# Plain first products in each MoE layer, sums of x made in the MoE, and two weight parts converted in single steps through the attention

## The chip, the cores and the metric

The kernel runs on one core of a Trainium2 chip. The metric is the device time in microseconds of one execution, the median of several. TensorE (PE) multiplies matrices and accumulates in PSUM; VectorE (DVE), ScalarE (ACT) and GpSimd (POOL) work element by element; SyncE (SP) issues DMAs, and so does POOL here. Each engine takes its instructions in the order in which they were written to its queue.

## What is computed

```python
scores = 0.125 * q @ k.T + bias(w1, b1, w2)      # 2 batches, 8 heads, 576 positions, head size 64
attn = softmax(scores); x = (attn @ v) as 1152 tokens x 512
x = ((x @ w_a) * (x @ w_b)) @ w_out              # first MoE layer, 512 -> 1536 -> 512
x = (silu(x @ w_gate) * (x @ w_val)) @ w_out2    # second MoE layer
```

The MoE weights arrive as 64-bit floats, which the kernel turns into 32-bit ones on the chip. All products keep 32-bit accuracy by splitting an operand into a high and a low part (`h` and `l` at the end of a name) and making three matmuls: high by high, high by low, low by high (`three`).

## The kernel before

**Attention.** The 1152 tokens are worked off in 20 steps: five row tiles t in the order 4, 0, 1, 2, 3, each for four pairs of heads p. A step of t=4 has one half step, the others two (one for each batch), so there are 36 half steps, counted here from 0. In each loop turn i, `first(i)` makes the scores in the PSUM tile `ps` (a single one), DVE adds the bias and finds the row extreme (the `es<-ps,bt` instruction, two in a half step), ACT takes the exponential; `second(i-1)` transposes on PE; `third(i-2)` multiplies by v, and `finish` scales the result by the inverse sums and splits it into x, high and low. Until turn 17 the loop also makes the position bias (`units`); then the pools of that work close and a pool for the weights opens in their place.

x has three token chunks of 384 (c = 0, 1, 2): `x0` (all four blocks of 128 rows), `x1` (blocks 2 and 3 only) and `x2`. For chunks 0 and 1 the MoE does not make eight block products but seven, after Winograd's scheme for 2 by 2 blocks; it needs four sums of x (`xt`, for two row pairs k) and four sums of weight blocks (`st`, the second half of `wh` and `wl`). In the attention `differences` makes `xt` on POOL, six elementwise operations and one subtraction of the high part at each of four places, with one ACT cast.

**Weights.** `Weights.part(layer, q, i)` fetches 1 MB (i = 0: w_a or gate, 1: w_b or value, 2: out) and converts it: ACT takes the absolute value, DVE makes four passes over 128x1024 elements (`m`), ACT casts the high part, DVE subtracts for the low part. For i below 2 DVE also makes the four sums (`s`), ACT casts them and DVE subtracts once more. `raw` and `m` have two buffers each; the high and low weights of i = 0 and i = 1 have one buffer each. Part (0,0,0) is made at the start of step 17 of the attention and part (0,0,1) at the start of the MoE in the program's text; DVE, ACT and POOL instructions are placed by a scheduler, which moved most of both into the last ten half steps.

**MoE.** Each layer has six q, each q two parts i of products. `products` makes the seven block products for chunks 0 and 1 in PSUM tiles `pa`, `pb`, `pd` with five DVE additions (`sum_of`); `plain` makes chunk 2 in `pv`. Between them `project` multiplies finished hidden values by the out weights into `po0` to `po3`, and DVE adds these to `acc`. `gate` copies on ACT, `value` multiplies and splits. PE's order is that of the program. At the end of layer 0, `project` empties its list of ten pieces, and `split` makes the new x from `acc`: casts on ACT, low parts on POOL, the four sums on DVE.

The order of the seven block products in `products`, which sets when PE needs `xt`, is: `x0` block, then `xt`[1], `xt`[0], `xt`[2], `x0`, `xt`[3], `x1`.

Of the kernel before, what the change touches and what calls it, by code (L numbers as in the profile page):

```python
# [2 lines left out]

# [6 lines left out]
F32 = mybir.dt.float32  # L10
F32R = mybir.dt.float32r
# [32 lines left out]
GROUP = 4  # L44
RAWS, MS, WOS, HS, GS, CS = 2, 2, 3, 12, 7, 3
# [27 lines left out]
class Activations:  # L73


    def __init__(self, pool):
        self.pool, self.late = pool, None
        self.layer()

    def layer(self):  # L80
        t = lambda n, tag: [self.pool.tile([P, n, CH], F32R, tag=f"{tag}{s}", name=f"{tag}{s}") for s in "hl"]
        self.x0, self.x1, self.x2 = t(NCC, "x0"), t(2, "x1"), t(NCC, "x2")
        if self.late:
            self.sums()
# [157 lines left out]
class Weights:  # L242
# [6 lines left out]
    def __init__(self, tc, wm, early):  # L249
        self.nc, self.early, self.pool, self.more, self.wm = tc.nc, early, None, None, wm  # L250
        self.got = {}

    def part(self, layer, q, i):
        nc = self.nc
        if i < 2:
            s, pool = i, (self.early, self.more)[i]
            wh, wl = (pool.tile([P, 8, 256], F32R, tag=f"w{x}{s}", name=f"w{x}{s}", bufs=1) for x in "hl")
        else:
            wh, wl = (self.more.tile([P, 4, 256], F32R, tag=f"wo{x}", name=f"wo{x}", bufs=WOS) for x in "hl")
        self.got[layer, q, i] = wh, wl  # L260
        raw = self.pool.tile([P, 2048], U32, tag="raw", name="raw", bufs=RAWS)
        nc.sync.dma_start(raw, self.wm[layer][q, i].bitcast(U32))
        lo, hi = (raw.rearrange("p (n t) -> p t n", t=2)[:, j] for j in range(2))
        mt = self.pool.tile([P, 4, 256], F32, tag="m", name="m", bufs=MS)
        m = mt.rearrange("p k f -> p (k f)")
        nc.scalar.activation(m, hi.bitcast(F32), AF.Abs)
        nc.vector.tensor_scalar(m, m, LEAST, MOST, op0=ALU.max, op1=ALU.min)
        t = m.bitcast(U32)
        nc.vector.tensor_scalar(t, t, 3, 0x3FFFFFF8, op0=ALU.logical_shift_left, op1=ALU.bitwise_and)
        nc.vector.scalar_tensor_tensor(t, lo, 29, t, op0=ALU.logical_shift_right, op1=ALU.bitwise_or)  # L270
        nc.vector.scalar_tensor_tensor(t, hi, 0xC0000000, t, op0=ALU.bitwise_and, op1=ALU.bitwise_or)  # L271
        nc.scalar.copy(wh[:, :4], mt)  # L272
        nc.vector.tensor_tensor(wl[:, :4], mt, wh[:, :4].bitcast(F32), op=ALU.subtract)  # L273
        if i < 2:
# [6 lines left out]
            nc.vector.tensor_tensor(wl[:, 4:], st, wh[:, 4:].bitcast(F32), op=ALU.subtract)  # L281


def attention(ctx, tc, a4, heads, share, bias, units, bias_d, x, weights, ident):
# [3 lines left out]
    with (  # L288
# [83 lines left out]
        def finish(p, s0, n, pu, rc):  # L372
            t1 = a2.tile([P, 256], F32, tag="t1", name="t1", bufs=4)
            nc.vector.tensor_tensor(t1[:, :n], pu[:, :n], rc[:, :n], op=ALU.mult)
            share.dve(n)
            share.dve(n)
            share.act(n)
            for c in range(NCH):
                a, e = max(s0, CH * c), min(s0 + n, CH * c + CH)
                if a >= e:  # L380
                    continue
                src, cols = t1[:, a - s0 : e - s0], slice(a - CH * c, e - CH * c)
                if c == 1:
                    kept[p] = src
                    if p < 2:
                        continue
                dh, dl = ((x.x0, x.x1, x.x2)[c][i][:, p - 2 if c == 1 else p, cols] for i in range(2))
                nc.scalar.copy(dh, src)
                nc.vector.tensor_tensor(dl, src, dh.bitcast(F32), op=ALU.subtract)
                if c == 1:  # L390
                    differences(p - 2, cols)

        def differences(k, cols):

            w = cols.stop - cols.start
            y0, y1 = kept[k], kept[k + 2]
            a, b = ([x.x0[i][:, r, cols].bitcast(F32) for i in range(2)] for r in (k, k + 2))
            tt = a4.tile([P, 4, 256], F32, tag="tt", name="tt", bufs=1)
            t = [tt[:, j, :w] for j in range(4)]
            add = nc.gpsimd.tensor_tensor  # L400
            add(t[0], y0, a[0], op=ALU.subtract)
            add(t[0], t[0], a[1], op=ALU.subtract)
            add(t[2], y1, y0, op=ALU.subtract)
            add(t[1], y1, t[0], op=ALU.subtract)
            add(t[3], b[0], t[1], op=ALU.subtract)
            add(t[3], t[3], b[1], op=ALU.add)
            dh, dl = (x.t[i][:, :, k, cols] for i in range(2))
            nc.scalar.copy(dh, tt[:, :, :w])
            nc.gpsimd.tensor_tensor(dl, tt[:, :, :w], dh.bitcast(F32), op=ALU.subtract)

        kept = {}
# [14 lines left out]
        def first(i):  # L426

            idx, p, t, b = halves[i]
            if b == 0:
# [41 lines left out]
        for i in range(len(halves) + 2):  # L471
# [20 lines left out]
def moe(tc, x, weights, out):  # L492
    nc = tc.nc
    pe = Pinned(tc, nc.tensor)
    with (
# [5 lines left out]
        weights.more = wpb  # L501
        weights.part(0, 0, 1)
        acc = [mp.tile([P, NCC, CH], F32, tag=f"acc{c}", name=f"acc{c}") for c in range(NCH)]
# [25 lines left out]
        def products(layer, q, i):  # L529
# [16 lines left out]
            product(a, 0, [v[:, :2] for v in x.x0], True)  # L546
# [11 lines left out]
            product(a, 1, [v[:, 2:] for v in x.x0], False)  # L558
# [5 lines left out]
            product(d, 7, x.x1, False)  # L564
# [3 lines left out]
        def plain(layer, q, i, j):  # L568
            w = weights.got[layer, q, i]
            ps = ph.tile([P, CH], F32, tag="pv", name="pv")  # L570
            for cc in range(NCC):
                ws = slice(P * (cc % 2), P * (cc % 2) + P)
                three(ps, [v[:, 2 * j + cc // 2, ws] for v in w], [v[:, cc] for v in x.x2], cc == 0, cc == NCC - 1)
            (gate, value)[i](layer, 2 * q + j, 2, ps, True)

        def project(layer, f0, f1, c, fc):
# [17 lines left out]
            if f1 == NFC and not layer:  # L594
                if c == 0:
                    x.layer()
                split(c)

        def split(c):
            dst = (x.x0, x.x1, x.x2)[c]  # L600
            for d in range(2 if c == 1 else 0, NCC):
                dh, dl = (v[:, d - 2 if c == 1 else d] for v in dst)
                nc.scalar.copy(dh, acc[c][:, d])
                nc.gpsimd.tensor_tensor(dl, acc[c][:, d], dh.bitcast(F32), op=ALU.subtract)
            if c == 1:
# [102 lines left out]
```

## Time and profile before

| | us |
|---|---|
| median of 3 runs | 683.8 (682.9 to 686.06) |
| the profiled execution | 688.58 |
| its span | 686.8 |
| PE busy | 630.1 (92%) |
| DVE busy | 557.0 (81%) |
| ACT busy | 347.8 (51%) |
| POOL busy | 50.2 (7%) |
| mean granted TensorE clock | 0.96 |

The profiled execution took 1.78 us more than its span from the first to the last instruction. Busy time of PE overstates its work, since matmuls overlap: the 128x384 ones show 0.34 us each and start every 0.17 us when nothing holds them up. So the number of matmuls in a stretch tells more than PE's busy time.

### The profile page before, as it was taken

The page shows a single profiled execution, that of the slowest core. Times are in us where ns is not written, and L with a number is a line of the kernel's source. Part 1 is how long each engine was busy: PE and PEld are TensorE (multiplying, and loading weights), DVE is VectorE, ACT ScalarE, POOL GpSimd, SP SyncE. Part 2 cuts the span into 40 slices and gives each one's busy share as a digit, 9 for nine tenths or more (in the row PEclk, how much of TensorE's full clock was granted, in tenths as well). Part 3 has the DMA queues.
Part 4 walks back from the last instruction along what each step waited for, and adds up shares of the span by engine and source line. Part 5 has one row for each costly group of instructions (what it writes and reads, how often), then busy time and mean ns, then how long its engine had stood idle before and what let it go on. Part 6 is the DMA issues. An engine that isn't in the chain of part 4 may idle for free.

```text
span 686.8 us, 11386 instructions
## 1 busy us (share of the span) xinstructions
PE 630.1 (92%) x4440; PEld 562.2 (82%) x4440; DVE 557.0 (81%) x1055; ACT 347.8 (51%) x672; POOL 50.2 (7%) x70
## 2 busy tenths in 40 slices
PE   5496999998958899999999999898999999999997
PEld 2254666577846799899999999788998999999997
DVE  6565789888879799989798989995999998887452
ACT  5486789875855644453544333444445445343210
POOL 4000000126230000000000000212000000000000
PEclk9789899998968999999999999998999999999999
DMA  8454364541444031333231312111113223110012
GB/s 326 169 181 149 114 187 138 155 138 57 126 167 163 36 124 61 123 112 113 84 123 62 108 52 86 62 62 62 63 61 123 72 113 123 62 62 1 0 47 93
DMA packets 19911, 71.42 MB, mean 104 GB/s; under 512 B 2096, under 2 KB 3776, under 8 KB 15248
## 3 DMA queue, kind: packets, MB, share of 16 engines
q1 hardware_dynamic: 17824, 63.21, 27.4%
q0 software_dynamic: 2032, 7.47, 3.2%
q8 instruction: 35, 0.57, 0.3%
q14 instruction: 20, 0.16, 0.1%
HBM read 57.42 MB, written 13.25 MB: 103 GB/s over the span
## 4 chain that ended last, share of the span: by engine, by line
PE 65%; DVE 19%; ACT 7%; DMA 5%; issue 3%; SPq 1%; ACTq 0%; DVEq 0%
PE po L98 20%; PE pv L98 12%; PE pb L98 9%; PE tp L98 6%; PE pd L98 6%; PE pa L98 5%; PE pu L98 4%; PE ps L98 3%; DMA bias_d<-bt 2%; ACT es L322 2%; DVE m L270 1%; ACT ee L329 1%; DVE m L271 1%; DVE wl L273 1%; ACT hd L155 1%
## 5 line engine op out<-in xcount | busy, mean ns | idle before, releaser
L98 PE MATMUL po<-gh,woh 128*128 128x384 f32 x288 | 97.4, 338 | 3.4 <-DVE acc L591 3.4
L98 PE MATMUL po<-gl,woh 128*128 128x384 f32 x288 | 97.2, 338 | 2.5 <-DVE gl L526 2.5
L98 PE MATMUL po<-gh,wol 128*128 128x384 f32 x288 | 97.0, 337 | 0.0
L525 ACT CAST gh<-g 128x384 fp32r<-128x384 f32 x72 | 35.2, 513 | 76.7 <-DVE g L523 76.5
L98 PE MATMUL tp<-hd,cs 128*32 128x264 f32 (+17 forms) x352 | 51.4, 551 | 18.1 <-DVE hd L153 15.4
L98 PE MATMUL pv<-x2h,wh 128*128 128x384 f32 x192 | 64.5, 336 | 0.4 <-ACT g L518 0.4
L316 DVE CUSTOM_DVE_ANT_0 es<-ps,bt 128x576 f32<-128x576 f32 x72 | 51.7, 751 | 15.6 <-DMA bt<-bias_d 10.0
L98 PE MATMUL pv<-x2l,wh 128*128 128x384 f32 x192 | 64.2, 334 | 0.0
L98 PE MATMUL pv<-x2h,wl 128*128 128x384 f32 x192 | 64.1, 334 | 0.0
L322 ACT ACTIVATE es<-es,nm 128x576 f32<-128x576 f32 x72 | 55.7, 775 | 9.0 <-DVE nm L316 8.8
L98 PEld LDWEIGHTS po<-gh,woh 128*128 128x128 f32 x288 | 54.6, 189 | 4.1 <-DVE acc L591 4.0
L98 PEld LDWEIGHTS po<-gl,woh 128*128 128x128 f32 x288 | 54.6, 190 | 3.6 <-DVE gl L526 3.5
L98 PEld LDWEIGHTS po<-gh,wol 128*128 128x128 f32 x288 | 54.5, 189 | 0.0
L98 PE MATMUL tp<-ident,es 128*128 128x128 f32 x324 | 48.7, 292 | 6.1 <-ACT es L322 3.9
L98 PE MATMUL pb<-xtl,wh 128*128 128x384 f32 x144 | 49.3, 343 | 4.2 <-DVE xtl L613 4.2
L98 PE MATMUL pb<-xth,wh 128*128 128x384 f32 x144 | 49.5, 344 | 2.8 <-DVE u L541 2.7
L98 PE MATMUL pu<-ee,vv 128*64 128x128 f32 (+1 forms) x800 | 51.6, 283 | 0.0
L98 PEld LDWEIGHTS tp<-hd,cs 128*32 128x32 f32 x352 | 14.2, 121 | 44.3 <-DVE hd L153 20.4
L98 PEld LDWEIGHTS tp<-ident,es 128*128 128x128 f32 x324 | 36.5, 147 | 15.9 <-ACT es L322 5.7
L272 ACT CAST wh<-m 128x1024 fp32r<-128x1024 f32 x24 | 25.3, 1052 | 47.9 <-PE pd L98 44.9
L98 PE MATMUL pb<-xth,wl 128*128 128x384 f32 x144 | 49.4, 343 | 0.0
L98 PEld LDWEIGHTS pu<-ee,vv 128*64 128x64 f32 x800 | 43.0, 148 | 6.3 <-issue 5.1
(124 smaller groups left out, 1512.4 us busy)
## 6 DMA issues: line engine op xcount, KB each, us to landing
raw<-in_wm SPq DMA_DIRECT2D x36, 1024.0 KB
bias_d<-bt SPq DMA_DIRECT2D x36, 295.5 KB
bt<-bias_d SPq DMA_DIRECT2D x32, 288.0 KB
vv<-in_vd POOLq DMA_DIRECT2D x4, 640.0 KB, 10.4
kr<-in_kd POOLq DMA_DIRECT2D x4, 576.0 KB, 7.3
bt<-bias_d SPq DMA_DIRECT2D x16, 144.0 KB
out_t<-acc SPq DMA_DIRECT2D x12, 192.0 KB
rawq<-in_qd POOLq DMA_DIRECT2D x16, 128.0 KB, 5.5
```

Source lines behind the costliest of these rows:

```text
L98: return self.tc.keep_in_program_order(getattr(self.engine, name)(*args, **kwargs))
L155: self.nc.scalar.activation(dst, self.LW[:, :n], AF.Relu, bias=self.bp[:, m : m + 1])
L270: nc.vector.scalar_tensor_tensor(t, lo, 29, t, op0=ALU.logical_shift_right, op1=ALU.bitwise_or)
L271: nc.vector.scalar_tensor_tensor(t, hi, 0xC0000000, t, op0=ALU.bitwise_and, op1=ALU.bitwise_or)
L272: nc.scalar.copy(wh[:, :4], mt)
L273: nc.vector.tensor_tensor(wl[:, :4], mt, wh[:, :4].bitcast(F32), op=ALU.subtract)
L316: nc.vector.tensor_tensor_reduce(out=es[:, j].rearrange("p (a j) -> p a j", a=2), in0=ps[:, j, :, :288], in1=bt[j].rearrange("p (a j) -> p ...
L322: nc.scalar.activation(es[:, j], es[:, j], AF.Exp, bias=nm, scale=-1.0, accum_out=sums[:, j : j + 1])
L329: nc.scalar.copy(dst, src)
L525: nc.scalar.copy(gh, g)
```

## The change

The diff has four parts.

- **Plain products.** For five (layer, q, i), named in `PLAIN`, chunks 0 and 1 are made like chunk 2, by `plain` with 72 matmuls in place of 66, going round `pa`, `pb`, `pd`, `pv`. These parts need no `xt` and no weight sums, and their weight part makes none.
- **Sums of x.** `differences` is gone. `x1` now has all four blocks, and `finish` keeps the unsplit result of chunks 0 and 1 in `acc0` and `acc1`, which now exist from the start. `sums`, which layer 1 had already, makes `xt` on DVE and ACT in layer 0 too, after part (0,0,0).
- **Weights ahead.** The raw data of parts (0,0,0) and (0,0,1) are fetched in turn 17. Their conversion is cut into twelve single instructions (five words, two split, five words), one put into each loop turn from 20 to 31 and pinned there.
- **Order.** `split(0,0,1)` comes at the start of the MoE; the parts for q = 1 are queued behind it.

```diff
+PLAIN = {(0, 0, 0), (0, 0, 1), (0, 1, 0), (1, 0, 0), (1, 0, 1)}
...
+        yield nc.scalar.activation(m, hi.bitcast(F32), AF.Abs)
+        yield nc.vector.tensor_scalar(m, m, LEAST, MOST, op0=ALU.max, op1=ALU.min)
+        yield nc.vector.tensor_scalar(t, t, 3, 0x3FFFFFF8, op0=ALU.logical_shift_left, op1=ALU.bitwise_and)
+        yield nc.vector.scalar_tensor_tensor(t, lo, 29, t, op0=ALU.logical_shift_right, op1=ALU.bitwise_or)
+        yield nc.vector.scalar_tensor_tensor(t, hi, 0xC0000000, t, op0=ALU.bitwise_and, op1=ALU.bitwise_or)
...
+        yield nc.scalar.copy(wh[:, :4], mt)
+        yield nc.vector.tensor_tensor(wl[:, :4], mt, wh[:, :4].bitcast(F32), op=ALU.subtract)
+        if i < 2 and (layer, q, i) not in PLAIN:
...
-                with tc.issue_after(load.ins):
-                    if idx == len(steps) - 3:
-                        weights.part(0, 0, 0)
...
-                weights.pool = x.late = ctx.enter_context(tc.tile_pool(name="wpa2", bufs=1, side="right"))
-                x.sums()
+                weights.pool = ctx.enter_context(tc.tile_pool(name="wpa2", bufs=1, side="right"))
+                weights.fetch(0, 0, 0)
+                weights.fetch(0, 0, 1)
+                ahead = chain(weights.words(0, 0, 0), weights.split(0, 0, 0), weights.words(0, 0, 1))
+            if i > len(MADE) + 1:
+                for op in islice(ahead, 1):
+                    units.tc.keep_in_program_order(op)
...
-            product(d, 7, x.x1, False)
+            product(d, 7, [v[:, 2:] for v in x.xs[1]], False)
...
+                    if (layer, q, i) in PLAIN:
+                        for n in range(2 * NCH):
+                            plain(layer, q, i, n % 2, n // 2, ("pa", "pb", "pd", "pv")[n % 4])
+                    else:
...
+                    if (layer, q, i) == (0, 0, 0):
+                        sums()
```

**DVE in the attention.** These are consecutive rows of DVE between the scores of half steps 30 and 31 in the kernel before. `m`, `s` and `wl` belong to the conversion of weights; `es` are the scores' instructions.

```order
L271 SCALAR_TENSOR_TENSOR m<-raw,m 128x1024
L269 TENSOR_SCALAR m<-m 128x1024
L367 COPY rc<-tp 128x256
L276 TENSOR_TENSOR s<-m 128x256
L278 TENSOR_TENSOR s<-m 128x256
L270 SCALAR_TENSOR_TENSOR m<-raw,m 128x1024
L273 TENSOR_TENSOR wl_2710<-m,wh_2709 128x1024
L277 TENSOR_TENSOR s<-s,m 128x256
L271 SCALAR_TENSOR_TENSOR m<-raw,m 128x1024
L279 TENSOR_TENSOR s<-m,s 128x256
L208 CAST qa<-rawq 128x256
L316 ISA es,nm<-ps,bt 128x576
```

And these are rows of DVE in the changed kernel between two half steps of the same part of the attention.

```order
L342 COPY ee<-tp 128x384
L382 COPY rc<-tp 128x256
L270 SCALAR_TENSOR_TENSOR m<-raw,m 128x1024
L209 CAST qa<-rawq 128x256
L331 ISA es,nm<-ps,bt 128x576
```

Nine conversion rows stood between two scores before; now one stands there, and there is never more than one.

**SP in the attention.** The DMA queue of SP around the last steps, before: `bt` is the bias of a step read back, `raw` a weight part.

```order
L194 DMA bias_d_60<-bt 16x8x591
L433 DMA bt<-bias_d_59 128x1x576 x6
L433 DMA bt<-bias_d_60 128x1x576 x4
L262 DMA raw<-in_wm 128x2048 x2
L433 DMA bt<-bias_d_60 128x1x576 x2
L262 DMA raw<-in_wm 128x2048 x2
```

In the changed kernel:

```order
L195 DMA bias_d_60<-bt 16x8x591
L256 DMA raw<-in_wm 128x2048 x2
L425 DMA bt<-bias_d_59 128x1x576 x6
L256 DMA raw<-in_wm 128x2048
L425 DMA bt<-bias_d_60 128x1x576 x8
```

The first two weight parts are now issued ahead of the last fourteen bias loads, which are seven steps' worth (six of tile 2, eight of tile 3), and a third stands between them.

**DVE at the change of layer.** Before, when the last pieces of chunk 0 come out of PSUM (`po`) at the end of layer 0:

```order
L591 TENSOR_TENSOR acc_3154<-po_4921,acc_3154 128x384
L267 TENSOR_SCALAR m<-m 128x1024
L276 TENSOR_TENSOR s<-m 128x256
L278 TENSOR_TENSOR s<-m 128x256
L591 TENSOR_TENSOR acc_3154<-po_4922,acc_3154 128x384
```

In the changed kernel:

```order
L585 TENSOR_TENSOR acc_73<-po_4886,acc_73 128x384
L268 TENSOR_SCALAR m<-m 128x1024
L585 TENSOR_TENSOR acc_73<-po_4887,acc_73 128x384
```

The two sums of weights are no longer ahead of the fourth addition; one pass over 128x1024 still is.

## Rows read from the trace of the kernel before

**Rows 1.** The page: busy time, share of the span and instructions of each engine.

```profile
PE 630.1 (92%) x4440; PEld 562.2 (82%) x4440; DVE 557.0 (81%) x1055; ACT 347.8 (51%) x672; POOL 50.2 (7%) x70
```

**Rows 2.** Windows by stage: busy time and instructions, granted clock, DMA.

```profile
core 0: us, PE busy (x) PEld busy (x) DVE busy (x) ACT busy (x) POOL busy (x), PEclk, DMA share, GB/s
147.00:235.00 88.00, 73.55 (x758) 60.19 (x759) 71.77 (x168) 59.19 (x139) 24.33 (x31) 0.86 0.36 116
234.00:300.00 66.00, 60.56 (x338) 58.25 (x337) 62.78 (x100) 28.39 (x42) 0.00 (x0) 1.00 0.27 96
300.00:436.00 136.00, 136.00 (x782) 135.88 (x782) 121.56 (x197) 56.42 (x85) 0.00 (x0) 1.00 0.27 93
436.00:480.00 44.00, 36.30 (x182) 34.82 (x181) 34.03 (x49) 17.52 (x31) 12.03 (x10) 0.88 0.13 49
```

**Rows 3.** DVE's timeline: the first scores of half steps 20, 25, 29, 33 and 35.

```profile
151.56 0.74 DVE L316 CUSTOM_DVE_ANT_0 es<-ps,bt 128x576 f32<-128x576 f32 x1
...
174.91 0.76 DVE L316 CUSTOM_DVE_ANT_0 es<-ps,bt 128x576 f32<-128x576 f32 x1 [1.05 <-PE ps L98]
...
189.27 0.76 DVE L316 CUSTOM_DVE_ANT_0 es<-ps,bt 128x576 f32<-128x576 f32 x1 [0.96 <-PE ps L98]
...
220.38 0.74 DVE L316 CUSTOM_DVE_ANT_0 es<-ps,bt 128x576 f32<-128x576 f32 x1
...
227.31 0.76 DVE L316 CUSTOM_DVE_ANT_0 es<-ps,bt 128x576 f32<-128x576 f32 x1 [1.14 <-PE ps L98]
```

**Rows 4.** POOL's and DVE's timelines, 155 to 177 us: two DVE operations, slow and normal.

```profile
154.99 2.37 POOL L409 TENSOR_TENSOR xtl<-tt,xth 128x1024 fp32r<-128x1024 f32 x1 [1.95 <-PE tp L98]
...
155.90 1.75 DVE L212 TENSOR_TENSOR qb<-rawq,qa 128x256 fp32r<-128x256 f32 x1
...
176.27 0.42 DVE L212 TENSOR_TENSOR qb<-rawq,qa 128x256 fp32r<-128x256 f32 x1
```

**Rows 5.** ACT's, DVE's and SP's timelines: the first weight part in the attention.

```profile
184.27 0.81 SPq L262 DMA_DIRECT2D raw<-in_wm  x2
...
193.35 1.12 ACT L266 ACTIVATE m<-raw 128x1024 f32<-128x1024 f32 x1 [4.33 <-DMA raw<-in_wm]
...
194.50 0.70 DVE L267 TENSOR_SCALAR m<-m 128x1024 f32<-128x1024 f32 x1 [3.79 <-ACT m L266]
...
205.04 1.21 DVE L270 SCALAR_TENSOR_TENSOR m<-raw,m 128x1024 uint32<-128x1024 uint32 x1
206.18 1.21 DVE L273 TENSOR_TENSOR wl<-m,wh 128x1024 fp32r<-128x1024 f32 x1
207.31 0.41 DVE L277 TENSOR_TENSOR s<-s,m 128x256 f32<-128x256 f32 x1
```

**Rows 6.** DVE's and PE's timelines in the first products of layer 0.

```profile
238.39 0.55 DVE L541 TENSOR_TENSOR u<-pb,s 128x384 f32<-128x384 f32 x1
...
238.99 0.44 PE L98 MATMUL pb<-xth,wh 128*128 128x384 f32 x1 [1.56 <-DVE u L541]
```

**Rows 7.** DVE's, PE's and POOL's timelines at the change of layer.

```profile
439.36 1.34 DVE L267 TENSOR_SCALAR m<-m 128x1024 f32<-128x1024 f32 x1
440.62 1.21 DVE L276 TENSOR_TENSOR s<-m 128x256 f32<-128x256 f32 x1
...
442.88 0.55 DVE L591 TENSOR_TENSOR acc<-po,acc 128x384 f32<-128x384 f32 x1
...
443.48 0.44 PE L98 MATMUL po<-gh,woh 128*128 128x384 f32 x1 [3.08 <-DVE acc L591]
...
445.07 0.52 PE L98 MATMUL po<-gl,woh 128*128 128x384 f32 x1
445.39 0.52 PE L98 MATMUL po<-gh,wol 128*128 128x384 f32 x1
...
466.07 2.45 POOL L604 TENSOR_TENSOR x2l<-acc,x2h 128x384 fp32r<-128x384 f32 x2 [0.23 <-ACT x2h L603]
...
466.43 0.69 PE L98 MATMUL pb<-xtl,wh 128*128 128x384 f32 x1 [4.24 <-DVE xtl L613]
```

More of the change, by code (lines that the diff above doesn't have):

```diff
@@ L77, in __init__ @@
         self.pool, self.late = pool, None
+        self.acc = [pool.tile([P, NCC, CH], F32, tag=f"acc{c}", name=f"acc{c}") for c in range(2)]
         self.layer()
     def layer(self):
[L81 to L84, printed above, removed]
+        t = lambda c: [self.pool.tile([P, NCC, CH], F32R, tag=f"x{c}{s}", name=f"x{c}{s}") for s in "hl"]
+        self.xs = [t(c) for c in range(NCH)]
     def sums(self):
@@ L249, in __init__, with fetch @@
     def __init__(self, tc, wm, early):
-        self.nc, self.early, self.pool, self.more, self.wm = tc.nc, early, None, None, wm
-        self.got = {}
-    def part(self, layer, q, i):
+        self.nc, self.pools, self.pool, self.wm = tc.nc, [early, None], None, wm
+        self.raw, self.whole, self.got = {}, {}, {}
+    def fetch(self, layer, q, i):
+        raw = self.pool.tile([P, 2048], U32, tag="raw", name="raw", bufs=RAWS)
+        self.nc.sync.dma_start(raw, self.wm[layer][q, i].bitcast(U32))
+        self.raw[layer, q, i] = raw
@@ new lines, in words @@
+    def words(self, layer, q, i):
+        nc = self.nc
+        raw = self.raw.pop((layer, q, i))
+        lo, hi = (raw.rearrange("p (n t) -> p t n", t=2)[:, j] for j in range(2))
+        mt = self.pool.tile([P, 4, 256], F32, tag="m", name="m", bufs=MS)
+        self.whole[layer, q, i] = mt
+        m = mt.rearrange("p k f -> p (k f)")
+        t = m.bitcast(U32)
+        yield nc.scalar.activation(m, hi.bitcast(F32), AF.Abs)
[3 more added lines that the diff above has]
+        yield nc.vector.scalar_tensor_tensor(t, hi, 0xC0000000, t, op0=ALU.bitwise_and, op1=ALU.bitwise_or)
@@ L254, in part, with split @@
+    def split(self, layer, q, i):
         nc = self.nc
         if i < 2:
[L256 to L257 removed]
+            wh, wl = (self.pools[i].tile([P, 8, 256], F32R, tag=f"w{x}{i}", name=f"w{x}{i}", bufs=1) for x in "hl")
         else:
[L259 removed]
+            wh, wl = (self.pools[1].tile([P, 4, 256], F32R, tag=f"wo{x}", name=f"wo{x}", bufs=WOS) for x in "hl")
@@ L260, in part @@
         self.got[layer, q, i] = wh, wl
[L261 to L274, printed above, removed]
+        mt = self.whole.pop((layer, q, i))
@@ L281, in part @@
             nc.vector.tensor_tensor(wl[:, 4:], st, wh[:, 4:].bitcast(F32), op=ALU.subtract)
+    def part(self, *key):
+        if key not in self.raw:
+            self.fetch(*key)
+        for _ in (*self.words(*key), *self.split(*key)):
+            pass
 def attention(ctx, tc, a4, heads, share, bias, units, bias_d, x, weights, ident):
@@ L500, in moe @@
     ):
-        weights.more = wpb
-        weights.part(0, 0, 1)
-        acc = [mp.tile([P, NCC, CH], F32, tag=f"acc{c}", name=f"acc{c}") for c in range(NCH)]
+        weights.pools[1] = wpb
+        begun = [*weights.split(0, 0, 1)]
+        acc, x.late = [*x.acc, mp.tile([P, NCC, CH], F32, tag="acc2", name="acc2")], mp
         gates, hiddens, pending, po = {}, {}, [], []
```

102 lines of the change are left out of this document (42 added, 60 removed).

## Prediction

> **What bounds the kernel now.** I read the page first. PE is busy for 92% of the span and DVE for 81% [rows 1], but a share over the whole span says little, so the next view was the windows by stage [rows 2]. In the middle of layer 0, from 300 to 436 us, PE starts 782 matmuls in 136.00 us, 0.174 us each, with a granted clock of 1.00: there PE alone is the bound, and nothing is to be gained but by fewer matmuls. Held against that rate, three stages lose time. From 234 to 300 us 338 matmuls should take 58.8 us of 66: 7.2 us are lost at full clock, while DVE is busy for 62.78. From 436 to 480 us 182 should take 31.7 us of 44: 12.3 us are lost, at a clock of 0.88. And before 235 us lies the end of the attention, at a clock of 0.86, where the matmuls are smaller, so that I measured it by its half steps.
>
> The timeline of DVE gives their beat by the first score instruction of each [rows 3]. From half step 25 to 29 it is 14.36 us for four, 3.59 each, and from 33 to 35 6.93 for two, 3.47 each. I take 3.5 as the undisturbed beat. From 20 to 35 the kernel took 75.75 us where fifteen such beats are 52.5: an excess of 23.2 us. It lies in two places: 5.9 us between half steps 20 and 25, and 17.1 us between 29 and 33.
>
> What happens there is in the timelines. In the first place POOL makes the sums of x, and DVE operations stretch: the subtraction for `qb` takes 1.75 us beside POOL's 2.37 us operation, and 0.42 when POOL is idle [rows 4]. In the second place the weight conversion stands on DVE and ACT in front of the scores. ACT waits 4.33 us for the raw data, issued 9.1 us before it starts, and DVE, whose first pass stands behind it, sits idle for 3.79 [rows 5]; the scores queue behind that pass. Then nine conversion operations stand between two scores, of which the passes and the subtraction take 1.21 us each by the record and start 1.13 us apart, and a sum takes 0.41 [rows 5].
>
> **The attention after the change.** Both causes go: no elementwise POOL work is left there, the raw data are fetched some 37 us earlier (near 147 us, not 184 [rows 5]), and the weight sums of the first parts are not made at all. What comes back, from the nearest rows:
>
> - Nine pinned DVE operations: two parts with two passes of 0.70 and two of 1.14, and one subtraction of 1.13 [rows 5], together 8.5 us. DVE waits 0.96 to 1.14 us for PE ahead of the first score of a step [rows 3], in about every second half step. By the order, five of the nine stand in that gap, 4.8 us, of which all but some 0.4 hides. The other four, 3.7 us, follow a split of x directly and stand in front of the next scores, with no gap to cover them. I count 4.1.
> - Three ACT operations of 1.12 us [rows 5], 3.4 in all. Whether ACT has room between two exponentials no row decides; between 0 and 3.4 I take half, 1.7.
> - Four more low parts of `x1` and four scalings cut in two, eight DVE operations more. By the 0.42 of `qb` [rows 4] at most 3.4; half of them are of 128 columns, and the scaling is only cut, so I take 1.4.
> - The bias loads that are now behind 2 MB of weights on SP. These took about 9 us to land [rows 5]. Issued when the bias work ends, near 147 us, they are done near 156, and the first load behind them is needed two beats after half step 20, at 158.6. It is hidden with some 2 us to spare; with contention it costs up to 3. I take 0.5.
>
> Sum: 7.7 us come back of 23.2, a gain of **15.5**. With everything exposed it is 18.3 back and a gain of 5; with everything hidden the gain is 23.
>
> At one place the Trainium skill prices this differently. Rows first: the 1.75 us operation starts while the POOL operation is under way and ends within 0.3 us of its end [rows 4]. The skill's page "SBUF — State Buffer" (section "SBUF: two separate sides") says that DVE and GpSimd share a port pair as an exclusive lock for a whole instruction, so that the loser does not slow down but stops. The trace agrees here. It speaks against another part of the change, for at the change of layer two more subtractions of `x1` go to POOL: by that rule each would stop DVE for its length, 1.2 us, and the total below would be a gain of 19.0 instead of 21.4. I count nothing for them, since DVE's list there has gaps of its own.
>
> **The start of layer 0.** Three plain parts bring 18 more matmuls, 3.1 us at 0.174. DVE is rid of five additions in each of three parts, 15 at 0.55 [rows 6], 8.2 us, and of the rest of the weight sums, four at 0.41 and two subtractions at 1.21 [rows 5], 4.1; it gets eight sums and eight low parts, 16 at 0.55, 8.8 us. So its list becomes some 3.5 us shorter, but does not get empty. New waits come with the plain form: the four PSUM tiles go round, and a value product in part (0,0,1) frees its tile only when DVE gets to it in order. Laying the rows of the order out with these durations, I find PE waiting about 2.0 us at the first `pa` of part (0,1,0), 1.2 at its fifth product, 1.5 at the start of (0,1,1), whose sums are just ready, and I add 1 for what follows: 5.7 us, in place of the 7.2 lost now. Net **1.6 us longer**. Without any waits it would be 4.1 shorter; with all 8.8 us of the new operations on the path, and the old waits halved, some 8 longer.
>
> **The change of layer.** Of the 12.3 us lost, 3.08 are the wait for the fourth addition, ahead of which DVE makes one pass of 1.34 and two sums of 1.21, and 4.24 the wait of the first `pb` for `xt` [rows 7]. The rest, 5.0 us, goes with the clock: after the waits matmuls start every 0.32 us [rows 7], at 0.88 mean clock [rows 2]. The change takes the two sums from in front of the addition, so 0.7 of the 3.08 stays. It takes `xt` from the first products: they need `x0`, `x1` and, after 48 matmuls or 8.3 us, `x2`. PE stood ready near 461.1 (six matmuls ahead of a wait of 4.24 that ended at 466.43), so `x2` is due at 469.4; its last low part ended at 468.5 [rows 7]. What is late next is therefore `x2`, by a margin of 0.9 us, and I leave 2.0 for it and for a remainder of low clock. The price is 12 more matmuls, 2.1 us. Sum: 12.3 − 0.7 − 2.0 − 2.1 = **7.5 gained**. The bounds are 10.2, with no waits left, and 3, if `x2` is late and the clock falls again.
>
> **The rest.** The order of DVE, ACT and PE up to half step 18 is the same but for names, and the middle of layer 0 has the same matmuls. I count nothing there, nor for the end of layer 1.
>
> Total: −15.5 + 1.6 − 7.5 = −21.4 us. From the profiled execution's 688.58 that gives 667.2. The runs shown have a median of 683.8, 4.8 us lower than the profiled one, and I apply the same difference: **662**.
>
> **Rivals.**
> - *The pinned operations give back most of what they take* (0.15). DVE is near its limit in the attention, and an in-order operation in front of the scores may delay the whole loop by its length. The gain there is then 5 to 8, in all some 12: 672. For it: DVE works 71.77 of 88 us there [rows 2]. Against it: much of that is the conversion itself and the stretched operations.
> - *DVE falls behind at the start of layer 0* (0.15). The sums move onto the engine that is busy for 62.78 of 66 us there [rows 2]; if all 8.8 us come onto PE's path, the stage is 8 longer, the total gain 15 and the time 669. The Trainium skill's page "Perfetto Trace Analysis" (section "Optimizing Scalar/DVE Operations") says that with DVE saturated it can pay to move work off to ScalarE or even GpSimd, and this edit goes the other way. Against it stands the shorter list worked out above.
> - *`x2` takes the place of `xt` at the change of layer* (0.12). PE stops at the fifth product, the clock falls as it does now, and the gain there is 3: 667.
> - *Everything hides* (0.10). The attention gives 23, layer 0 loses nothing, the change of layer gives 9: 652 or a little less.
> - *Slower* (0.03). If the waits in the first three plain parts bring the clock down and hold it, their 216 matmuls start every 0.32 us in place of 0.174 [rows 7], 31 us more; against the 23 gained elsewhere the kernel ends at 692. It decides from about 160 matmuls at the low clock on. Against it: the clock stayed at 1.00 from 234 to 300 us in spite of 7.2 lost us [rows 2].
>
> **Chances and range.** The forecast has 0.45. Its own range is 657 to 667. For 8 in 10 I take 651 to 674, which leaves out the slower case, the worst of the first two rivals added up, and part of the case in which everything hides. A measurement of this kernel can tell about 0.5%, 3.4 us, from no change: faster 0.95, same 0.02, slower 0.03.
>
> **What would show it.** In the changed profile the beat of half steps 20 to 35 should be about 4.0 us on average, with no DVE operation above 1.3 us and no wait of ACT for `raw`; PE should reach the first `pa` of the MoE near 218 us. The granted clock there should be above 0.95. In the first 66 us of the MoE DVE should still be nearly full and PE's waits should name DVE's `g`, `xtl` or ACT's `g`, some 6 us in all. At the change of layer no wait of PE should exceed 2 us, the clock should stay near 1.00, and POOL's `x2l` should end just before the fifth plain product. The prediction is wrong if the beat in the attention stays above 4.5 us, if the bias loads of half step 22 are late behind the weights, or if PE's clock falls in the plain parts.

## The result and the profile after

| | before | after |
|---|---|---|
| median, us | 683.35 (680.46 to 686.06, 4 runs) | 660.6 (659.57 to 661.25, 4 runs) |
| ratio | | 0.9666, interval 0.9624 to 0.9708 |
| the profiled execution and its span, us | 688.58, 686.8 | 659.57, 657.8 |

The forecast was 662; the time came out 22.75 us below that of before, where 21.4 were summed up. The total hides several errors of its terms, and that it came so near is in part luck. The rest of this text is about them.

The page after, first line, and the windows by stage (columns as in [rows 2]). The stages are the last part of the attention from 128 us on, the first 66 us of layer 0, its middle, and the change of layer in two pieces:

```profile
PE 619.2 (94%) x4470; PEld 554.6 (84%) x4470; DVE 535.3 (81%) x1029; ACT 347.6 (53%) x678; POOL 30.5 (5%) x44
```

```profile
128.00:215.00 87.00, 80.46 (x925) 63.48 (x923) 70.44 (x196) 68.78 (x167) 3.76 (x7) 1.00 0.44 141
215.00:281.00 66.00, 63.44 (x363) 62.21 (x360) 62.43 (x99) 32.82 (x53) 0.00 (x0) 1.00 0.31 112
281.00:415.00 134.00, 134.00 (x775) 134.00 (x774) 119.29 (x193) 53.65 (x83) 0.00 (x0) 1.00 0.27 95
415.00:441.00 26.00, 24.59 (x138) 23.64 (x138) 24.82 (x32) 11.56 (x21) 11.17 (x9) 1.00 0.12 42
441.00:459.00 18.00, 17.79 (x101) 17.18 (x101) 14.71 (x23) 9.81 (x17) 4.64 (x4) 1.00 0.17 59
```

Beside [rows 2]: the granted clock is 1.00 in all five, where it was 0.86 and 0.88 at the end of the attention and at the change of layer. The first 66 us of layer 0 now hold 363 matmuls instead of 338. The middle is the same, 0.173 us each.

**Attention.** DVE's timeline: the first scores of half steps 20, 21, 25 and 35, as in [rows 3], the `qb` of [rows 4] and one pinned operation.

```profile
149.02 0.75 DVE L331 CUSTOM_DVE_ANT_0 es<-ps,bt 128x576 f32<-128x576 f32 x1
...
155.77 0.76 DVE L331 CUSTOM_DVE_ANT_0 es<-ps,bt 128x576 f32<-128x576 f32 x1 [1.82 <-PE ps L99]
...
157.13 0.42 DVE L213 TENSOR_TENSOR qb<-rawq,qa 128x256 fp32r<-128x256 f32 x1
...
169.81 1.22 DVE L271 SCALAR_TENSOR_TENSOR m<-raw,m 128x1024 uint32<-128x1024 uint32 x1
170.94 0.75 DVE L331 CUSTOM_DVE_ANT_0 es<-ps,bt 128x576 f32<-128x576 f32 x1
...
208.40 0.76 DVE L331 CUSTOM_DVE_ANT_0 es<-ps,bt 128x576 f32<-128x576 f32 x1 [1.21 <-PE ps L99]
```

From half step 20 to 35 it is 59.38 us, a beat of 3.96 (before 75.75 us). But one beat, 20 to 21, takes 6.75, and the other fourteen 3.76 on average. What PE waited for there is ACT, and ACT for the raw weights, which SP had issued 4.9 us earlier (SP's, ACT's and PE's timelines):

```profile
146.60 0.82 SPq L256 DMA_DIRECT2D raw<-in_wm  x2
```

```profile
151.51 1.12 ACT L267 ACTIVATE m<-raw 128x1024 f32<-128x1024 f32 x1 [2.28 <-DMA raw<-in_wm]
```

```profile
153.06 0.44 PE L99 MATMUL tp<-ident,rw 128*128 128x128 f32 x2 [3.21 <-ACT ee L344]
153.43 1.31 PE L99 MATMUL pu<-ee,vv 128*64 128x128 f32 x20
```

**Start of layer 0.** PE's waits in the MoE up to 300 us (in total, times, longest); the first stood at the first `pa` of part (0,1,0), at 242.00:

```profile
PE pa L99 <- DVE g L517: 1.7, 1, 1.7
PE pb L99 <- DVE c L535: 0.6, 1, 0.6
PE pb L99 <- ACT g L512: 0.3, 1, 0.3
```

**Change of layer.** PE's timeline holds two short waits, both for an addition into `acc`, and none at the first part of layer 1 (before 3.08 and 4.24 [rows 7]); in the second part there is one of 0.21 for a gate value:

```profile
419.85 0.45 PE L99 MATMUL po<-gh,woh 128*128 128x384 f32 x1 [0.70 <-DVE acc L585]
...
427.51 0.44 PE L99 MATMUL po<-gh,woh 128*128 128x384 f32 x1 [0.62 <-DVE acc L585]
...
436.33 0.33 PE L99 MATMUL pa<-x0h,wh 128*128 128x384 f32 x1
```

DVE's and POOL's timelines there. Passes that take 0.68 and 1.22 us elsewhere take 1.45 and 1.92 while POOL subtracts:

```profile
417.88 1.45 DVE L268 TENSOR_SCALAR m<-m 128x1024 f32<-128x1024 f32 x1
419.25 0.54 DVE L585 TENSOR_TENSOR acc<-po,acc 128x384 f32<-128x384 f32 x1
419.72 1.02 DVE L269 TENSOR_SCALAR m<-m 128x1024 uint32<-128x1024 uint32 x1
420.77 1.92 DVE L270 SCALAR_TENSOR_TENSOR m<-raw,m 128x1024 uint32<-128x1024 uint32 x1
422.72 1.93 DVE L271 SCALAR_TENSOR_TENSOR m<-raw,m 128x1024 uint32<-128x1024 uint32 x1
```

```profile
417.76 5.80 POOL L594 TENSOR_TENSOR x0l<-acc,x0h 128x384 fp32r<-128x384 f32 x4 [236.51 <-ACT x0h L593]
...
442.86 3.60 POOL L594 TENSOR_TENSOR x2l<-acc,x2h 128x384 fp32r<-128x384 f32 x3 [0.82 <-ACT x2h L593]
```

### The profile page after: what moved, and what is told of

Same layout as the page of the kernel before. It is cut to its first block, busy times and chain, and to the rows that moved or that the text cites. A ratio compares the mean times of both kernels' runs of the same rounds, so it can differ in the third digit from the quotient of the medians.

```text
span 657.8 us, 11385 instructions
## 1 busy us (share of the span) xinstructions
PE 619.2 (94%) x4470; PEld 554.6 (84%) x4470; DVE 535.3 (81%) x1029; ACT 347.6 (53%) x678; POOL 30.5 (5%) x44
## 4 chain that ended last, share of the span: by engine, by line
PE 65%; DVE 15%; ACT 8%; DMA 8%; issue 3%; SPq 0%; POOL 0%; ACTq 0%; POOLq 0%; DVEq 0%
PE po L99 20%; PE pv L99 11%; PE pb L99 10%; PE pa L99 7%; PE pd L99 6%; PE tp L99 5%; PE pu L99 4%; DMA bt<-bias_d 3%; PE ps L99 2%; ACT es L337 2%; DVE m L270 2%; DVE m L271 2%; DMA bias_d<-bt 2%; ACT ee L344 2%; DMA kr<-in_kd 1%
## 5 line engine op out<-in xcount | busy, mean ns | idle before, releaser
L99 PE MATMUL pv<-x2h,wh 128*128 128x384 f32 x152 | 50.8, 334 | 0.0
L99 PE MATMUL pv<-x2l,wh 128*128 128x384 f32 x152 | 50.8, 334 | 0.0
L99 PE MATMUL pv<-x2h,wl 128*128 128x384 f32 x152 | 50.8, 334 | 0.0
L99 PE MATMUL pu<-ee,vv 128*64 128x128 f32 (+1 forms) x800 | 48.3, 271 | 0.0
L267 ACT ACTIVATE m<-raw 128x1024 f32<-128x1024 f32 x36 | 41.5, 1152 | 11.8 <-DVE wl L282 4.3
L99 PE MATMUL tp<-ident,es 128*128 128x128 f32 x324 | 45.7, 281 | 2.0 <-ACT bt L162 1.6
L99 PEld LDWEIGHTS pu<-ee,vv 128*64 128x64 f32 x800 | 40.3, 141 | 5.8 <-issue 5.3
L270 DVE SCALAR_TENSOR_TENSOR m<-raw,m 128x1024 uint32<-128x1024 uint32 x36 | 44.6, 1238 | 0.2
L271 DVE SCALAR_TENSOR_TENSOR m<-raw,m 128x1024 uint32<-128x1024 uint32 x36 | 44.5, 1237 | 0.1
L99 PEld LDWEIGHTS tp<-ident,es 128*128 128x128 f32 x324 | 34.4, 140 | 10.6 <-ACT bt L162 3.5
```

The lines of the kernel that those rows point to most:

```text
L99: return self.tc.keep_in_program_order(getattr(self.engine, name)(*args, **kwargs))
L267: yield nc.scalar.activation(m, hi.bitcast(F32), AF.Abs)
L270: yield nc.vector.scalar_tensor_tensor(t, lo, 29, t, op0=ALU.logical_shift_right, op1=ALU.bitwise_or)
L271: yield nc.vector.scalar_tensor_tensor(t, hi, 0xC0000000, t, op0=ALU.bitwise_and, op1=ALU.bitwise_or)
```

## The experiments

The changed kernel was run again beside the later ones: 659.64 us (658.72 to 661.07). In its profile the beat of half steps 20 to 21 was 8.87 us instead of 6.75, with the same order of instructions. This and the start of the kernel make single profiles differ by some us. So each profile is cut into pieces at rows that all have: the first score of half steps 6, 20 and 35, PE's first `pa` of the MoE (6.69 us behind half step 35 in every profile), and the end of the span.

| kernel | median, us | half step 6 at | 6 to 20 | 20 to 35 (of it 20 to 21) | MoE: first `pa` to end |
|---|---|---|---|---|---|
| before | 683.35 | 78.65 | 72.91 | 75.75 (2.98) | 452.80 |
| after | 660.6 | 76.98 | 72.04 | 59.38 (6.75) | 442.71 |
| after, again | 659.64 | 75.70 | 72.01 | 62.20 (8.87) | 442.70 |
| e1_pool_back | 663.21 | 74.99 | 73.27 | 64.19 (8.13) | 442.66 |
| e2_bunched | 663.93 | 74.39 | 71.96 | 66.52 (3.46) | 442.74 |
| e8_unpinned | 665.04 | 76.80 | 76.14 | 61.84 (4.82) | 442.73 |
| e3_two_plain | 666.81 | 75.41 | 72.01 | 59.06 (6.44) | 451.63 |
| e4_no_l1 | 669.24 | 76.97 | 72.01 | 60.61 (7.99) | 452.22 |
| e5_turn22 | 654.47 | 73.13 | 72.01 | 56.94 (3.46) | 442.73 |
| e6_dve_low | 658.15 | 74.12 | 71.98 | 62.05 (9.07) | 441.66 |
| e9_both | 653.6 | 80.20 | 71.99 | 56.83 (3.45) | 441.69 |

The last column repeats within 0.1 us wherever the MoE was not edited, so a difference of 1 us in it is a measurement. The start, up to half step 6, is the piece that no edit touches and that varies most, from 73.13 to 80.20.

**e0_again: the changed kernel once more.**

> The changed kernel itself, once more, to stand beside the next three on the same chip. All theories expect what it showed, 659 to 662 us, with MoE's first matmul 60 to 67 us after the scores of half step 20.

The time is as expected; the first `pa` came 68.9 us behind the scores of half step 20, above the 60 to 67 expected. The raw data again came late: ACT waited 2.31 us for it and PE 3.24 for ACT, as in the first profile. What differs is what PE did behind the wait. Here are the same two groups of PE, and the clock of the 5 us around them:

```profile
151.78 0.69 PE L99 MATMUL tp<-ident,rw 128*128 128x128 f32 x2 [3.24 <-ACT ee L344]
152.40 2.40 PE L99 MATMUL pu<-ee,vv 128*64 128x128 f32 x20
```

```profile
152.00:157.00 5.00, 5.00 (x37) 4.06 (x37) 0.85 (x2) 2.02 (x6) 0.00 (x0) 0.50 0.45 131
```

Twenty matmuls that took 1.31 us at full clock in the first profile take 2.40 at a granted clock of 0.50 (the lower level, 1.2 GHz). After a like wait, the beat was 6.44 and 6.75 us in the two profiles in which the clock stayed at 1.00, and 7.99 to 9.07 in the four in which it fell. So the late weights cost 2.9 to 5.6 us over a beat of 3.5.

**e1_pool_back: idle work on POOL at the four old places.** The results go to a tile that nobody reads; nothing waits for them.

```diff
-                src = a2.tile([P, 256], F32, tag="t1", name="t1", bufs=4)
+                src = a2.tile([P, 256], F32, tag="t1", name="t1", bufs=2)
...
+                if c == 1 and p >= 2:
+                    idle_sums(p - 2, cols)
...
+            for j, (i0, i1) in enumerate(((y0, a[0]), (y0, a[1]), (y1, y0), (y1, a[0]), (b[0], y0), (b[1], y0))):
+                nc.gpsimd.tensor_tensor(tt[:, j % 4, :w], i0, i1, op=ALU.subtract)
+            nc.gpsimd.tensor_tensor(tt[:, :, :w], x.acc[0][:, :, :w], x.xs[0][0][:, :, :w].bitcast(F32), op=ALU.subtract)
```

> The changed kernel, with POOL elementwise work put back at the same four places and of the same sizes as in the kernel before (six operations of 256 or 128 columns, one of 1024 or 512), whose results nothing uses; DVE's and ACT's lists are unchanged, and the t1 tile has two buffers, not four. Theory: POOL's mere presence stretched DVE's operations, 5.9 us of the 23.2 us of excess in the attention. Then half steps 19 to 25 get some 4 to 7 us longer, single DVE operations of 0.42 us take 0.8 to 1.8 there, and the kernel takes 665 to 668 us. Rival: the gain came from DVE's and ACT's shorter lists and POOL alone does no harm: within 1 us of the changed kernel.

It took 663.21 us, ratio to before 0.9697 (0.9663 to 0.9731). The piece before half step 20 is 1.2 us longer than after's, and half steps 21 to 35 take 56.06 us instead of 52.63 (after) and 53.33 (again): 4.0 to 4.7 us in all, of which the times show 2.6 to 3.6. That is less than the 665 to 668 us expected, and more than its rival's 1 us. A pass that takes 0.68 us elsewhere takes 1.21 beside POOL in these rows of DVE and POOL:

```profile
160.73 1.21 DVE L268 TENSOR_SCALAR m<-m 128x1024 f32<-128x1024 f32 x1
161.86 0.74 DVE L331 CUSTOM_DVE_ANT_0 es<-ps,bt 128x576 f32<-128x576 f32 x1
```

```profile
160.49 0.90 POOL L413 TENSOR_TENSOR tt<-acc,x0h 128x256 bf16<-128x256 f32 x1
161.47 2.72 POOL L414 TENSOR_TENSOR tt<-acc,x0h 128x1024 bf16<-128x1024 f32 x1
```

POOL slows the attention though nobody waits for its results, by the stretch of DVE: from half step 20 to 35 DVE is busy for 52.75 us with 138 instructions, where the same 138 take 49.53 and 49.42 in the two profiles of the changed kernel. It costs less here than the 5.9 us that the prediction read between half steps 20 and 25 of before: POOL's operations from 148.13 to 152.7 us fall into the time in which the half step waits for the late weights anyway.

**e2_bunched: the parts fetched and converted where before had them.** No weight sums, and the scheduler places the operations.

```diff
+                with tc.issue_after(load.ins):
+                    if idx == len(steps) - 3:
+                        weights.part(0, 0, 0)
...
-                weights.fetch(0, 0, 0)
-                weights.fetch(0, 0, 1)
-                ahead = chain(weights.words(0, 0, 0), weights.split(0, 0, 0), weights.words(0, 0, 1))
-            if i > len(MADE) + 1:
-                for op in islice(ahead, 1):
-                    units.tc.keep_in_program_order(op)
...
-        begun = [*weights.split(0, 0, 1)]
+        weights.fetch(0, 0, 1)
+        begun = [*weights.words(0, 0, 1), *weights.split(0, 0, 1)]
```

> The changed kernel, with the two first weight parts fetched and converted where the kernel before had them in its text (part 0,0,0 at the start of step 17, part 0,0,1 at the start of the MoE), in the scheduler's places; the operations themselves are those of the changed kernel, without the weight sums. Theory: what the spread saves is the stall behind the late data and the bunch of operations in front of the scores. ACT waits some 4 us for raw again, two or three half steps take 7 to 9 us in place of 3.5, and the kernel is 7 to 11 us slower than the changed one, 668 to 672. Rival: the saved weight sums were the whole gain and the place does not matter: within 2 us of the changed kernel.

It took 663.93 us, ratio 0.9705 (0.9664 to 0.9746). Thirteen of the fifteen beats are between 2.9 and 4.4, but two take 9.76 and 10.01 us. In the first, DVE waits for ACT, which starts on `raw` 9.3 us after its issue on SP (before 9.1 [rows 5]), and the scores stand behind:

```profile
183.83 0.69 DVE L268 TENSOR_SCALAR m<-m 128x1024 f32<-128x1024 f32 x1 [6.91 <-ACT m L267]
184.44 0.75 DVE L331 CUSTOM_DVE_ANT_0 es<-ps,bt 128x576 f32<-128x576 f32 x1
```

That is the picture of [rows 5], with 12.8 us above two beats of 3.5; here, though, the profile names nothing that ACT waited for, so that it was the raw data is read from the like distance alone. Spreading is worth 4.3 to 7.1 us of half steps 20 to 35, and 3.3 to 4.3 of the time. That is less than the 7 to 11 expected, since the spread form had a late fetch of its own: against e5 below, where that is mended, it is 9.6 us of half steps 20 to 35 and 9.5 of the time.

**e8_unpinned: the same cutting, without the pin.**

```diff
-                    units.tc.keep_in_program_order(op)
+                    pass
```

> The changed kernel without the pin on the twelve conversion operations: the same fetch, the same text, but the scheduler places them, and puts both parts' operations into half steps 18 to 21, right behind the fetch. Theory: what counts is where the operations stand against the data: ACT and DVE then wait for raw with the scores behind them, 5 to 9 us for the two parts, and the rest stands in a bunch; 5 to 10 us slower than the changed kernel, 666 to 671. Rival: fetching ahead is what counts and the order does not: within 2 us.

It took 665.04 us, ratio 0.9717 (0.9664 to 0.9771). The scheduler moved the operations forward. The first pass now stands in front of half step 20 and waits 3.83 us for ACT. Two others stand ahead of the small reciprocal `rs`, which ACT needs for `rw` and PE for its next transpose (DVE's and PE's timelines):

```profile
152.33 0.69 DVE L268 TENSOR_SCALAR m<-m 128x1024 f32<-128x1024 f32 x1 [3.83 <-ACT m L267]
...
165.01 1.21 DVE L282 TENSOR_TENSOR wl<-m,wh 128x1024 fp32r<-128x1024 f32 x1
166.14 1.22 DVE L271 SCALAR_TENSOR_TENSOR m<-raw,m 128x1024 uint32<-128x1024 uint32 x1
167.28 0.17 DVE L373 RECIPROCAL rs<-rs 128x4 f32<-128x4 f32 x1
```

```profile
167.99 0.69 PE L99 MATMUL tp<-ident,rw 128*128 128x128 f32 x2 [6.05 <-ACT rw L375]
168.61 2.40 PE L99 MATMUL pu<-ee,vv 128*64 128x128 f32 x20
```

PE waits 6.05 us and then works at a granted clock of 0.50, 2.40 us for the 1.31 of twenty matmuls. The beats from 19 to 23 are 7.71, 4.82, 5.43 and 9.22 us; behind them they lie between 3.0 and 4.1. The pin is worth 4.4 to 5.4 us, at the lower end of the 5 to 10 expected: it keeps an operation near its own turn, behind the arrival of its data and at most one in a half step.

**e3_two_plain and e4_no_l1: fewer plain parts.** In e3, (0,1,0) has the seven products and makes weight sums again; in e4, layer 1 has.

```diff
-PLAIN = {(0, 0, 0), (0, 0, 1), (0, 1, 0), (1, 0, 0), (1, 0, 1)}
+PLAIN = {(0, 0, 0), (0, 0, 1), (1, 0, 0), (1, 0, 1)}
```

```diff
-PLAIN = {(0, 0, 0), (0, 0, 1), (0, 1, 0), (1, 0, 0), (1, 0, 1)}
+PLAIN = {(0, 0, 0), (0, 0, 1), (0, 1, 0)}
```

> The changed kernel with part (0,1,0) made by the seven block products again, with its weight sums: 6 matmuls less, 1.0 us. Theory: xt and the weight sums are then wanted 12.5 us earlier, while DVE is full; by DVE's list xt is ready some 38 us after the MoE begins, and the part would start at 25, so that PE waits 8 to 12 us, and less DVE work in the plain part is lost too: 6 to 11 us slower than the changed kernel, 667 to 671. Rival: the scheduler puts the sums earlier and DVE has room for them: then 0 to 2 us slower or up to 1 us faster.

> The changed kernel with plain products only in layer 0: parts (1,0,0) and (1,0,1) are made by the seven block products again, with their weight sums, and 12 matmuls are saved, 2.1 us. Theory: the wait of the first pb for xt comes back with 4 us and the low clock behind it with 1 to 2, while the wait for the fourth addition comes back with the weight sums in front of it: 4 to 7 us slower than the changed kernel, 664 to 668. Rival: xt is no longer late, since layer 0 ends with less in DVE's list: then the 12 matmuls saved make it 2 us faster, 658.5.

e3 took 666.81 us, ratio 0.9772 (0.9724 to 0.982), e4 669.24, ratio 0.9788 (0.9749 to 0.9826). Their MoE is 8.9 and 9.5 us longer than after's, nearly as long as that of before. PE's timelines, e3 at the first (0,1,0) products and e4 at the change of layer:

```profile
240.31 0.44 PE L99 MATMUL pa<-x0h,wh 128*128 128x384 f32 x1 [1.41 <-DVE g L517]
...
248.47 0.69 PE L99 MATMUL pb<-xth,wh 128*128 128x384 f32 x1 [4.97 <-ACT xth L606]
...
250.14 0.69 PE L99 MATMUL pb<-xtl,wh 128*128 128x384 f32 x1 [0.98 <-DVE xtl L607]
```

```profile
424.17 0.44 PE L99 MATMUL po<-gh,woh 128*128 128x384 f32 x1 [3.07 <-DVE acc L585]
...
447.77 0.69 PE L99 MATMUL pb<-xtl,wh 128*128 128x384 f32 x1 [4.69 <-DVE xtl L607]
```

Both show what a plain part buys: for six more matmuls, 1 us, the sums have a part's time to be made in. The low clock comes back with the waits: it is 0.71 from 246 to 262 us in e3 and 0.57 from 446 to 454 in e4. The waits of e4 are those of [rows 7] back in their places, 3.07 for 3.08 and 4.69 for 4.24, and the first has the sums of weights in front of it again (DVE's timeline):

```profile
421.30 1.21 DVE L285 TENSOR_TENSOR s<-m 128x256 f32<-128x256 f32 x1
422.44 1.21 DVE L287 TENSOR_TENSOR s<-m 128x256 f32<-128x256 f32 x1
423.57 0.54 DVE L585 TENSOR_TENSOR acc<-po,acc 128x384 f32<-128x384 f32 x1
```

Without layer 1's plain parts the kernel is 8.6 us slower than with them, more than the 4 to 7 expected, so the rival expected of e4 falls. And layer 0, 1.8 us shorter than before with three plain parts, is 7 longer than before with two: there PE waits for `xth` and `xtl`, the sums of x that DVE and ACT now make, and only the third plain part gives these the time.

**e5_turn22: the pinned operations two turns later.** Turns 22 to 33 instead of 20 to 31.

```diff
-            if i > len(MADE) + 1:
+            if i > len(MADE) + 3:
```

> The changed kernel with the twelve pinned operations in turns 22 to 33, not 20 to 31, the fetch as it was. In the changed kernel ACT's first pinned operation waits 2.28 us for raw and the beat from half step 20 to 21 is 6.75 us. Theory: that wait is all that is left of the late data, and two turns later they have landed; the beat there returns to 3.5 and the attention is 2.5 to 3.5 us shorter, 657 to 658.5 us. Rival: the scores of that half step are late for another reason, the bias loads behind the 2 MB of weights; then the beat stays near 6.7 somewhere in half steps 20 to 23 and the time within 1 us of the changed kernel's.

It took 654.47 us (652.61 to 656.76), ratio 0.9570 (0.9520 to 0.9621), 5.2 below the changed kernel beside it. ACT's first operation on `raw` no longer waits, as its row shows, and the beat from 20 to 21 is 3.46. What is late next stands two half steps on, on DVE: the bias loads that SP issued behind the 2 MB of weights, both scores of half step 22 (ACT's and DVE's timelines).

```profile
152.27 1.14 ACT L267 ACTIVATE m<-raw 128x1024 f32<-128x1024 f32 x1
```

```profile
152.88 0.76 DVE L331 CUSTOM_DVE_ANT_0 es<-ps,bt 128x576 f32<-128x576 f32 x1 [0.58 <-DMA bt<-bias_d]
154.72 0.76 DVE L331 CUSTOM_DVE_ANT_0 es<-ps,bt 128x576 f32<-128x576 f32 x1 [1.07 <-DMA bt<-bias_d]
```

The gain is above the 2.5 to 3.5 us expected of the wait alone. By the pieces, half steps 20 to 35 are 2.4 us shorter than in the first profile of the changed kernel, in which the clock stayed at 1.00 behind the wait, and 5.3 shorter than in the second, in which it fell. So the clock, which stays at 1.00 there now, can give the rest; in how many of the executions behind the medians it fell is not known.

**e6_dve_low: the low parts of x at the change of layer on DVE.**

```diff
-                    nc.gpsimd.tensor_tensor(dl, acc[c][:, d], dh.bitcast(F32), op=ALU.subtract)
+                    nc.vector.tensor_tensor(dl, acc[c][:, d], dh.bitcast(F32), op=ALU.subtract)
```

> The changed kernel with the twelve low parts of x at the change of layer made by DVE, not POOL. In the changed kernel DVE's passes beside POOL's subtractions take 1.45 and 1.9 us in place of 0.68 and 1.21, some 5 us in all. Theory of the shared port: DVE's list does not get longer, since 12 subtractions at 0.47 add 5.6 us and as much stretching goes; PE's waits there (0.70 and 0.62) change by less than 1 us and the time stays within 1.5 us of the changed kernel's. Rival, POOL takes work off DVE as one would think: PE's waits at the change of layer grow by 3 us or more and the kernel takes 664 or more.

It took 658.15 us, ratio 0.9622 (0.9578 to 0.9666), 1.5 below the changed kernel beside it, just inside what the theory allowed. The MoE is 1.04 us shorter. The passes are short again, in DVE's timeline:

```profile
420.08 0.68 DVE L269 TENSOR_SCALAR m<-m 128x1024 uint32<-128x1024 uint32 x1
420.68 0.55 DVE L594 TENSOR_TENSOR x0l<-acc,x0h 128x384 fp32r<-128x384 f32 x1
421.15 1.22 DVE L270 SCALAR_TENSOR_TENSOR m<-raw,m 128x1024 uint32<-128x1024 uint32 x1
422.40 1.22 DVE L271 SCALAR_TENSOR_TENSOR m<-raw,m 128x1024 uint32<-128x1024 uint32 x1
```

A subtraction of 0.55 us on DVE replaces one that took POOL 1.45. Four of those (5.80 us) had stretched four passes by 2.5 us together (6.32 for 3.80). Over the whole MoE DVE is busy for 369.78 us instead of 371.89, although it makes twelve subtractions more: POOL's twelve had cost it more by the stretch than it now spends on making them. Of PE's two waits for `acc` at the change of layer the first is gone, and only this one is left in PE's timeline:

```profile
427.54 0.45 PE L99 MATMUL po<-gh,woh 128*128 128x384 f32 x1 [0.64 <-DVE acc L585]
```

**e9_both: e5 and e6 together.**

> The two edits that helped put together: conversion pinned two turns later (turns 22 to 33), and the twelve low parts of x at the change of layer made on DVE. Beside the changed kernel the first gave 5.2 us (654.47 against 659.64) and the second 1.5 (658.15). They lie 200 us apart in the run and share no wait, so if each is worth that by itself they add up: 659.6 - 5.2 - 1.5 = 652.9, between 651 and 655. Rival: the second was only the spread of the start-up between executions, and the time is that of the first alone, 654 to 656. The profile should show passes of 0.68 and 1.22 us on DVE at the change of layer, no ACT wait for raw, and bias waits of some 1.6 us behind the weights near half step 22.

It took 653.6 us (652.46 to 659.37, 6 runs), ratio 0.9578 (0.9546 to 0.9609): within the spread of e5. The pieces tell more than the median: 20 to 35 is 56.83 as in e5, and the MoE 441.69 as in e6, so both gains are there in full. The bias waits are 1.04 us instead of e5's 1.65. The profiled execution was the longest of the six, 659.37 us, and its half step 6 came at 80.20. This is the fastest median of the study, 29.7 us below before and 6 to 7 below the change.

## Why the prediction was right, step by step

- **The attention, −15.5.** Measured: −16.4 in the first profile, −13.55 in the second. The causes were right. The pieces divide it: e2, which has neither POOL's work nor the weight sums, is 9.2 us shorter than before, and the changed kernel, by the spreading, another 4.3 to 7.1. Of the 9.2, 5.75 lie in half steps 20 to 25, where before had POOL's work and no weight work yet, and 3.5 from 25 to 35, where it had the sums of weights and the rest of POOL's work. So the missing sums are worth 3.5 us at most by this comparison; they were not tried alone. e1 gives POOL 4.0 to 4.7 us (1.2 of it ahead of half step 20). But two of the steps behind the sum were wrong, in opposite directions. "The raw data are fetched some 37 us earlier" was read as no wait of ACT: the step that failed is that the first use had moved too, to turn 20, only some 2.6 us behind the issue, and the data takes 4.9. By the prediction's own figure, landing near 156 us, the first pinned operation of turn 20 had to wait. That cost 2.9 to 5.6 us. Against it, what comes back was put at 7.2 us without the bias loads, and half steps 21 to 35 took 52.63 to 53.33 us for fourteen beats, 3.6 to 4.3 above 49: the pinned operations there hid more than the prediction granted them. The beat of 3.96, forecast as about 4.0, comes of these two errors and is luck; in the second profile it is 4.15.
- **The bias loads** cost nothing that the changed kernel's profile shows: DVE waits for none of them there, everything being late by the wait for the weights. e5 removes that cover and 1.65 us of waits appear, inside the range of 0 to 3, whose upper end came from no row.
- **PE at the first `pa`**, forecast near 218 us, was at 215.09 and 216.60. The first is 18.9 us earlier than before: 16.4 of the fifteen beats, 0.9 between half steps 6 and 20, where POOL already worked before, and 1.67 of the start.
- **The start of layer 0, +1.6.** From the first `pa` of the MoE to the last `pd` of layer 0 it is 198.0 us (215.09 to 413.10), before 199.8 (234.00 to 433.78): −1.8. The place and the name of the longest wait were right (`pa` of (0,1,0) for `g`, 1.67 for 2.0). The term is the sum of waits, 5.7 forecast and 2.6 named in the profile: the wait of 1.2 at the fifth product, laid out from durations like the others, did not come, and for the 1.5 at (0,1,1) there is one of 0.3.
- **The change of layer, −7.5.** From that last `pd` to the first `pa` of layer 1 is 23.2 us, before 26.5; from there to the end 221.5, before 226.5. Together −8.3. The wait of 0.7 for the addition, the clock at 1.00 and the missing wait for `xt` came as forecast. `x2l` ended at 446.46 by POOL's row; its last block was due near 446.2 (48 matmuls and nine more at 0.173 behind 436.33), so it was just in time, and the 2.0 us left for it were not needed.
- **The lock of the two engines' ports.** By the Trainium skill's page "SBUF — State Buffer" (section "SBUF: two separate sides") two more subtractions on POOL would have stopped DVE for 2.4 us, an estimate from the 1.2 us of one. The trace agrees only in part: beside the 5.80 us of POOL's first four subtractions the four passes lengthened by 2.5 us, so DVE was slowed there and not stopped all that time. PE's total shows 1.04 us when all twelve subtractions go from POOL to DVE (e6), which is the stretch less what DVE then spends on them. The prediction counted nothing for the two added ones, and what they cost was not tried alone.
- **The total** came nearer than its terms, and that is luck. The three terms measured give −26.5 us with the first profile and −23.7 with the second, where −21.4 was summed up. From one profiled execution to the other it is −29.0, so that the 667.2 us forecast for it was 7.6 too high. The median of before, from which 662 was taken, is 5.2 us below its profiled execution, but the median after is 1.0 above its own. The pieces of the profiles from half step 6 on give −27.3 us with the first profile and −24.5 with the second, where the medians give −22.75. The late half step 6 of the profiled execution of before can explain some of that. With one profile of before, the rest stays open.

The rivals: pinned operations did not give back most of what they take, DVE did not fall behind at layer 0 (e3 shows by how much it would have), and `x2` was on time. That everything hides did not come true for the changed kernel; only e9, with two edits more, comes near to its 652 us, at 653.6.

## What to carry to other kernels

A transfer that is moved ahead must be judged by the distance from issue to first use; here the use was moved ahead with it, and the queue of an engine that takes its instructions in order stopped behind it. Where single profiles differ by some us, cut each at rows that all have and compare pieces: the MoE of this kernel repeated within 0.1 us while its two medians lay 1 us apart. And a plain form with more matmuls can pay as a stretch of work that needs nothing, placed where the operands of the shorter form are still being made.

## What was not expected of the hardware

- During a wait of PE of 2.9 to 3.4 us at half step 21 the granted clock fell to 0.50, for 3.4 to 6.8 us, in four profiles and stayed at 1.00 in two, at the same place of the same order of PE's instructions. The length of the wait does not separate them: 2.90 and 3.21 us where it stayed, 2.92, 3.24, 3.39 and 3.44 where it fell. What decides it is open.
- Up to half step 6 the same order of instructions took 73.13 to 80.20 us, and from 6 to 20 72.0 in all the profiles that leave that stretch alone. The granted clock between 0 and 40 us was 0.87 in e5 (73.13) and 0.83 in e9 (80.20), but 0.79 in e3 (75.41), so it does not by itself decide how long the start takes. What does is open.
- DVE's passes at the change of layer took 1.5 to 2.1 times their length beside POOL's subtractions, and one in e1 1.8 times.
